# Every fourth K/V half transfer in two parts, of 120 and of 8 partitions

## The chip, the core and the metric

The kernel runs on one core of a Trainium2 chip: TensorE (PE) for matrix products, VectorE (DVE), ScalarE (ACT), GpSimd (POOL), and SyncE (SP), which here issues every DMA. 16 DMA engines carry the transfers between HBM and the core's SBUF, a memory of 128 partitions. The metric is the device time of one execution in microseconds (us), lower is better.

## What is computed

Two layers of decoding attention, each followed by a dense block, for 8 sequences with one new token each (model width 448). The attention has 16 query heads over 8 K/V heads of width 256, and sees the last 1024 of 4096 cached positions:

```python
k = jnp.repeat(k_cache[:, :, Sk - W:, :], rep, axis=1)
v = jnp.repeat(v_cache[:, :, Sk - W:, :], rep, axis=1)
scores = jnp.einsum("bhqd,bhkd->bhqk", q, k) * (Dh ** -0.5)
p = _softmax(scores, axis=-1)
o = jnp.einsum("bhqk,bhkd->bhqd", p, v)
...
x = x + _A_ref(_layernorm(x, axis=-1), A_k_cache, A_v_cache, A_wq, A_wo)
x = x + _B_ref(_layernorm(x, axis=-1), B_w1, B_w2)
x = x + _A_ref(_layernorm(x, axis=-1), A_k_cache, A_v_cache, A_wq, A_wo)
x = x + _B_ref(_layernorm(x, axis=-1), B_w1, B_w2)
```

`_B_ref` is a product with `w1`, a SiLU and a product with `w2`. Both layers use the same caches and weights, so the data of one sequence can be read once and used by both.

## The kernel before

The kernel is a plan: helpers record tasks (a few instructions of one engine, with an estimated duration and the names of what they read and write), `Plan.schedule` puts the tasks of PE, DVE, ACT and POOL in an order by these estimates, and `Plan.emit` writes the orders out with semaphore waits. SP's tasks keep the order in which they were recorded. Each DMA task names a semaphore of its own kind (for K and V one per slot and half). `emit` counts 16 for each DMA on it (L215), the DMA adds 16 when it has landed (L266), and whoever needs the data waits for the count (L261).

For each of the 8 sequences (`b`), the K data of 8 heads and then the V data of 8 heads come in. One head's K or V for 1024 positions is 512 KB and fills one of `R = 29` slots in SBUF, of 128 partitions by 2048 bf16. `load_k` (L522) and `load_v` (L528) fetch it as two halves of 128 partitions by 1024 elements, one row of 2 KB for each partition; for K a half is half of every row, for V it is half of the positions. That makes 8 x 16 x 2 = 256 halves of 256 KB. The weights (wq, wo, w1, w2) are loaded once, wq first and the others after the first sequence's K and V.

Two things hold a transfer of the stream back. `dma` (L476) makes it wait for the landing of the transfer recorded `AHEAD = 7` before it (L478), so that about seven are in flight. And `pump` (L981) records a load into a slot only behind the compute that used the slot before: both layers' scores for K, both layers' PV products for V.

Compute for one sequence: `layer1` transposes the K halves in place on DVE (L998), then come scores (L672), softmax, PV (L731) and the output projection (L774, L780); `layer2` runs the dense block of the first layer, the query projection (L877) and the second attention over the same slots. The dense block behind the second layer is done for seven sequences together near the end, and for the last sequence at the very end.

Of the kernel before, what the change touches and what calls it, by code (L numbers as in the profile page):

```python
# [32 lines left out]
class Plan:  # L33
# [10 lines left out]
    def add(self, eng, fns, reads=(), writes=(), dur=0.1, prio=0.0, name="", n_bytes=0, dma_key=None):  # L44
        if not isinstance(fns, (list, tuple)):
            fns = [fns]
        if eng == "pool":
            writes = list(writes) + ["pool_serial"]
        t = Task(eng, list(fns), dur, prio, name, n_bytes)
        t.idx = len(self.tasks)  # L50
        t.sem = dma_key
        deps = {}

        def dep(o, raw):
            if o is not t:
                deps[o.idx] = (o, raw or (deps[o.idx][1] if o.idx in deps else False))

        for k in reads:
            if k in self.last_w:
                dep(self.last_w[k], True)  # L60
            if k[0] == "bank":
                for r in self.readers.get(k, ()):
                    if r.eng != eng:
                        dep(r, False)
        for k in writes:
            if k in self.last_w:
                dep(self.last_w[k], True)
            for r in self.readers.get(k, ()):
                dep(r, False)
        for k in reads:  # L70
            if k not in writes:
                self.readers.setdefault(k, []).append(t)
        for k in writes:
            self.last_w[k] = t
            self.readers[k] = []
        t.deps = deps
        self.tasks.append(t)
        return t
# [116 lines left out]
    def emit(self):  # L195
        nc = self.nc
        order = self.order
        mk = nc.alloc_semaphore
        eng_sem = {e: mk("s_" + e) for e in ("pe", "dve", "act", "pool")}
        dsem, dcount = {}, {}  # L200
        for t in self.tasks:
            for o, raw in t.deps.values():
                if o.eng != t.eng or o.eng == "sp" or (raw and t.eng in ("dve", "act", "pool")):
                    o.users += 1
        cnt = {e: 0 for e in eng_sem}
        for e in eng_sem:
            for t in order[e]:
                if t.users:
                    cnt[e] += 1
                t.sem, t.val = e, cnt[e]  # L210
        for t in order["sp"]:
            if t.sem not in dsem:
                dsem[t.sem] = mk("s_d_" + t.sem)
                dcount[t.sem] = 0
            dcount[t.sem] += 16  # L215
            t.val = dcount[t.sem]
        handles = dict(eng_sem)
        handles.update(dsem)
        known = {e: {} for e in order}
        waits_of = {}  # L220
        pos = {e: 0 for e in order}
        n_done = 0
        total = len(self.tasks)
        emitted = set()
        while n_done < total:
            moved = False
            for e in order:
                while pos[e] < len(order[e]):
                    t = order[e][pos[e]]
                    if any(o.idx not in emitted for o, _ in t.deps.values()):  # L230
                        break
                    kn = known[e]
                    need = {}
                    for o, raw in t.deps.values():
                        if o.eng == e and e != "sp" and not (raw and e in ("dve", "act", "pool")):
                            continue
                        if need.get(o.sem, (0, None))[0] < o.val:
                            need[o.sem] = (o.val, o)
                    waits = []
                    for s, (v, o) in sorted(need.items(), key=lambda kv: -len(kv[1][1].vc)):  # L240
                        if kn.get(s, 0) >= v:
                            continue
                        waits.append((s, v))
                        kn[s] = v
                        for s2, v2 in o.vc.items():
                            if kn.get(s2, 0) < v2:
                                kn[s2] = v2
                    waits_of[t.idx] = waits
                    t.vc = dict(kn)
                    t.vc[t.sem] = max(t.vc.get(t.sem, 0), t.val)  # L250
                    emitted.add(t.idx)
                    pos[e] += 1
                    n_done += 1
                    moved = True
            assert moved, "the order of the engines is circular"

        def run_all(e):
            def f(eng):
                for t in order[e]:
                    for s, v in waits_of[t.idx]:  # L260
                        eng.wait_ge(handles[s], v)  # L261
                    ins = None
                    for fn in t.fns:
                        ins = fn(eng)
                    if e == "sp":
                        ins.then_inc(handles[t.sem], 16)  # L266
                    elif t.users:
                        ins.then_inc(handles[e], 1)
                if e == "sp":
                    eng.wait_ge(handles[order["sp"][-1].sem], order["sp"][-1].val)  # L270
            return f

        with nc.Block(no_gpsimd_drain=True) as block:
            block.sync(run_all("sp"))
            block.tensor(run_all("pe"))
            block.vector(run_all("dve"))
            block.scalar(run_all("act"))
            block.gpsimd(run_all("pool"))


def bass_interleave_layers__sliding_block_cached__dense_activation_silu__decode_kernel(
# [3 lines left out]
    _, HKV, SK, DH = A_k_cache.shape  # L285
# [3 lines left out]
    W = min(4096, max(256, SK // 4))  # L289
    S0 = SK - W  # L290
    P = 128
# [12 lines left out]
    HQ = 4.0 / D  # L304
    R = 29
    AHEAD = 7
    NJ = 3

    x2 = A_x.rearrange("b s d -> (b s) d")
# [7 lines left out]
    slots = [sb(f"slot{i}", [P, 2048], BF16) for i in range(R)]  # L317
# [158 lines left out]
    def dma(fn, writes, n_bytes, key, reads=(), rate=395e3, ahead=None):  # L476
        t = add("sp", fn, reads=reads, writes=writes, n_bytes=n_bytes, dma_key=key, dur=n_bytes / rate, name=key)
        if ahead and len(started) >= ahead:  # L478
            t.deps[started[-ahead].idx] = (started[-ahead], True)
        started.append(t)  # L480
# [37 lines left out]
    W1_R = [("w1", c) for c in range(5)] + ["w1_pad"]  # L518

    slot_of = {}  # L520

    def load_k(s, b, kvh):  # L522
        src = A_k_cache[b, kvh, S0:SK, :].rearrange("(p u) d -> p (u d)", p=P)
        for h in range(2):
            dma(lambda e, h=h: e.dma_start(slots[s][:, 1024 * h:1024 * h + 1024], src[:, 1024 * h:1024 * h + 1024]),
                [("slot", s, h)], W * DH, "slot%d_%d" % (s, h), ahead=AHEAD)

    def load_v(s, b, kvh):  # L528
        src = A_v_cache[b, kvh, S0:SK, :].rearrange("(h p u) d -> h p (u d)", h=2, p=P)
        for h in range(2):  # L530
            dma(lambda e, h=h: e.dma_start(slots[s][:, 1024 * h:1024 * h + 1024], src[h]),  # L531
                [("slot", s, h)], W * DH, "slot%d_%d" % (s, h), rate=378e3, ahead=AHEAD)

    def wq_l(o, i):
        if i < 3:
# [237 lines left out]
    def rows_part(i0, n, first, last, w_sb, rhs, reads, name):  # L773
        pe([lambda e, i=i, c=c: e.matmul(  # L774
            bank[XB][32 * c:32 * c + 1, 0:D], rhs(i), w_sb[:, i * D:(i + 1) * D],
            start=(first and i - i0 < 4), stop=(last and i - i0 >= n - 4), tile_position=(0, 32 * c),
            skip_group_check=True) for i in range(i0, i0 + n) for c in [i % 4]], reads, bk(XB), (D, 4), name)
# [203 lines left out]
    def pump():  # L981
        while n_load[0] < len(seq) and (n_load[0] < R or seq[n_load[0] - R] in freed):
            x = seq[n_load[0]]
            slot_of[x] = n_load[0] % R
            n_load[0] += 1
            (load_k if x[1] == "k" else load_v)(slot_of[x], x[0], x[2])
            if x == (0, "v", 7):
                load_wo()
                load_w1()
                load_w2()  # L990

    def layer1(b):
# [11 lines left out]
        for h in range(2):  # L1004
            rows_part(8 * h, 8, h == 0, False, wo_sb, lambda i: oT1[:, i % 2, i // 2:i // 2 + 1],
                      [("oT1", k) for k in (2 * h, 2 * h + 1)] + WO_R, "wor")
        pv_rows(b, 0, 1, oT1, "oT1", SC[0], 0, 0, NJ)
        if NJ:
            rows_part(16, 4*NJ, False, NJ == 3, wo_sb, lambda i: oT1[:, i % 2, i // 2:i // 2 + 1],
                  [("oT1", k) for k in range(4,4+NJ)] + WO_R, "wor")  # L1010
        for kvh in range(4+NJ, 8):
            pv_cols(b, 0, kvh, oT1, "oT1")
# [69 lines left out]
```

## Time and profile before

| | us |
|---|---|
| time, median of 3 runs | 270.83 (269.54 to 271.26) |
| the profiled execution | 269.46 |
| span of its trace, first to last instruction | 267.7 |
| PE busy | 210.4 (79%) |
| DVE busy | 153.8 (57%) |
| ACT busy | 75.0 (28%) |
| POOL busy | 21.0 (8%) |

The profile is of one execution. Its page gives busy times by engine, a picture of the span in 40 equal slices of 6.7 us (each digit the busy share in tenths), the DMA queues, and the chain of work that ended last, followed back from the last instruction. Busy digits of the DMA row are the mean over the 16 DMA engines; it can read a little over 1. "SPq" is the time SP spends on issuing. "x256" behind a group is a count. A wait is written as who waited, then an arrow to who released it, then the total, the number of times and the longest.

### The profile page before, as it was taken

To read this page: it belongs to the slowest core of one execution; us is meant where nothing else is said; L and a number is where in the kernel's file an instruction comes from. 1 tells how busy PE (TensorE), PEld (TensorE's weight loads), DVE (VectorE), ACT (ScalarE), POOL (GpSimd) and SP (SyncE) were. 2 spreads that over 40 slices of the span, in tenths; PEclk is the share of its full clock that TensorE was granted. 3 is DMA by queue.
4 is the path that set the end of the run, shared out by engine and by line. 5 is a ranking of instruction groups with operands and counts; after the bars stand their busy time and mean duration, and the time that the engine had idled before them with its cause. 6 is when DMAs were issued, how large, how long until landed. Compare 5 with 4: busy or idle time off the path is not lost.

```text
span 267.7 us, 11667 instructions
## 1 busy us (share of the span) xinstructions
PE 210.4 (79%) x5178; PEld 135.7 (51%) x5178; DVE 153.8 (57%) x453; ACT 75.0 (28%) x259; POOL 21.0 (8%) x115
## 2 busy tenths in 40 slices
PE   0054684778789878987899889769889985999996
PEld 0052341354457545654566556446555752667763
DVE  7289110156927880986498479818773891334233
ACT  2004310211053314332432533143343312430322
POOL 6100000002000200020002001000200020003000
PEclk9999999689999997999999999999999999999689
DMA  6999999999999999997999998999999998100000
GB/s 248 343 403 392 385 333 401 319 334 354 351 351 298 373 349 348 376 366 249 353 382 348 315 369 296 375 303 354 383 311 337 343 351 272 39 6 2 5 2 4
DMA packets 41123, 78.44 MB, mean 293 GB/s; under 512 B 4321, under 2 KB 7345, under 8 KB 40689
## 3 DMA queue, kind: packets, MB, share of 16 engines
q1 hardware_dynamic: 41072, 77.69, 82.3%
q8 instruction: 41, 0.67, 1.0%
q14 instruction: 10, 0.07, 0.1%
HBM read 77.67 MB, written 0.01 MB: 290 GB/s over the span
## 4 chain that ended last, share of the span: by engine, by line
PE 41%; DMA 35%; DVE 9%; SPq 6%; ACT 5%; issue 3%; ACTq 0%
DMA slot<-in_A_k_cache_dram 24%; PE bank L731 7%; PE bank L672 7%; DMA slot<-in_A_v_cache_dram 6%; DMA w2o<-in_A_wo_dram 6%; PE bank L774 5%; PE bank L877 5%; DVE slot L998 5%; SPq L531 4%; PE bank L833 3%; PE bank L780 3%; PE bank L1045 2%; DVE qT L882 2%; PE bank L558 2%; PE bank L888 2%
## 5 line engine op out<-in xcount | busy, mean ns | idle before, releaser
L998 DVE STREAM_TRANSPOSE slot<-slot 128x512 uint32<-128x512 uint32 x128 | 81.7, 684 | 11.4 <-DMA slot<-in_A_k_cache_dram 11.4
L672 PE MATMUL bank<-slot,qbd 128*8 128x256 bf16 x1024 | 38.2, 283 | 9.1 <-DVE mseg L678 4.5
L731 PE MATMUL bank<-slot,pT_sb 128*2 128x256 bf16 x960 | 41.7, 297 | 3.8 <-DMA slot<-in_A_v_cache_dram 2.7
L672 PEld LDWEIGHTS bank<-slot,qbd 128*8 128x8 bf16 x1024 | 23.4, 86 | 19.9 <-DVE mseg L678 6.4
L1045 PE MATMUL bank<-wq_sb,cols_b 128*32 128x512 bf16 (+2 forms) x269 | 29.7, 422 | 0.0
L731 PEld LDWEIGHTS bank<-slot,pT_sb 128*2 128x2 bf16 x960 | 22.4, 88 | 12.3 <-issue 5.2
L656 ACT ACTIVATE qbd<-q1s 32x128 bf16<-32x128 bf16 x32 | 10.1, 314 | 51.6 <-PE bank L672 51.0
L717 DVE RECIPROCAL rl_sb<-bank 128x16 f32<-128x16 f32 x16 | 4.1, 256 | 33.1 <-PE bank L712 33.0
L736 ACT ACTIVATE o_sb<-bank 128x256 bf16<-128x256 f32 x32 | 12.3, 383 | 35.9 <-PE bank L731 20.1
L774 PE MATMUL bank<-w2o,oT 128*1 128x448 bf16 x256 | 15.6, 359 | 6.9 <-issue 4.3
L877 PE MATMUL bank<-wq_sb,xn 128*4 128x256 bf16 (+1 forms) x384 | 18.7, 307 | 1.4 <-issue 0.9
L790 ACT ACTIVATE qT<-bank 128x448 bf16<-128x448 f32 x17 | 9.3, 544 | 28.0 <-PE bank L774 28.0
L566 POOL TENSOR_SCALAR rstd<-va 128x1 int32<-128x1 int32 x8 | 1.5, 192 | 195.3 <-ACT va L823 195.3
L678 DVE TENSOR_REDUCE mseg<-bank 128x1 f32<-128x256 f32 x32 | 12.8, 405 | 6.2 <-PE bank L672 6.0
L882 DVE STREAM_TRANSPOSE qT<-bank 128x256 f32<-128x256 f32 (+1 forms) x24 | 11.9, 521 | 7.7 <-PE bank L877 7.7
L833 PE MATMUL bank<-xbt,w_sb 128*128 128x32 bf16 x504 | 15.8, 177 | 0.1
L833 PEld LDWEIGHTS bank<-xbt,w_sb 128*128 128x128 bf16 x504 | 14.0, 97 | 2.0 <-ACT xbt L801 1.7
L742 DVE TENSOR_TENSOR oT<-bank,rl_sb 128x16 bf16<-128x16 f32 (+1 forms) x32 | 6.0, 186 | 15.0 <-PE bank L738 14.9
L1045 PEld LDWEIGHTS bank<-wq_sb,cols_b 128*32 128x32 bf16 (+2 forms) x269 | 9.1, 105 | 8.4 <-issue 5.6
L774 PEld LDWEIGHTS bank<-w2o,oT 128*1 128x1 bf16 x256 | 5.3, 82 | 12.3 <-DVE oT L742 4.8
L819 DVE SCALAR_TENSOR_TENSOR va<-bank,m 128x1 f32<-128x1 f32 x9 | 1.3, 149 | 17.0 <-ACT m L817 16.8
L695 ACT ACTIVATE qT<-bank,mb,rstd 128x256 bf16<-128x256 f32 x16 | 8.7, 565 | 7.0 <-DVE mb L691 6.8
(164 smaller groups left out, 267.6 us busy)
## 6 DMA issues: line engine op xcount, KB each, us to landing
slot<-in_A_k_cache_dram SPq DMA_DIRECT2D x128, 256.0 KB, 5.3
slot<-in_A_v_cache_dram SPq DMA_DIRECT2D x128, 256.0 KB, 5.2
w2o<-in_A_wo_dram SPq DMA_DIRECT2D x2, 1792.0 KB, 12.7
wq_sb<-in_A_wq_dram SPq DMA_DIRECT2D x3, 1024.0 KB, 7.0
w2o<-in_B_w_dram SPq DMA_DIRECT2D x1, 1568.0 KB, 15.5
w_sb<-in_B_w_dram SPq DMA_DIRECT2D x3, 448.0 KB, 13.9
wq_sb<-in_A_wq_dram SPq DMA_DIRECT2D x2, 256.0 KB, 10.3
w_sb<-in_B_w_dram SPq DMA_DIRECT2D x1, 128.0 KB, 12.7
```

Of the source, the lines that this page charges most:

```text
L531: dma(lambda e, h=h: e.dma_start(slots[s][:, 1024 * h:1024 * h + 1024], src[h]), [("slot", s, h)], W * DH, "slot%d_%d" % (s, h), rate=378e ...
L656: act(lambda e, q=q: e.activation(qbd[0][32 * q:32 * q + 32].rearrange("p k c (q r) -> p (k c) q r", r=2)[:, :, q, :], q1s[32 * t:32 * t + ...
L672: fns.append(lambda e, cb=cb, par=par, j=j, kvh=kvh, kv=kv: e.matmul(bank[sc][32 * j:32 * j + 8, k2 * 256:(k2 + 1) * 256], qbd[layer][:, k ...
L678: dve(lambda e: e.tensor_reduce(mseg[layer][:, k2:k2 + 1], bank[sc][:, k2 * 256:(k2 + 1) * 256], AX.X, ALU.max, negate=True), bk(sc), [("m ...
L731: fns.append(lambda e, qh=qh, uh=uh, j=j, vv=vv: e.matmul(bank[ob][32 * j:32 * j + 2, c0:c0 + DH], p_col(ei, k2, j, qh, uh), vv, start=(qh ...
L736: act(lambda e: e.activation(o_sb[oi][:], bank[ob][:, c0:c0 + DH], ACTF.Copy), bk(ob), [("o", oi)], 0.385, "oevh" if ob == OB[0] else "oev ...
L774: pe([lambda e, i=i, c=c: e.matmul(bank[XB][32 * c:32 * c + 1, 0:D], rhs(i), w_sb[:, i * D:(i + 1) * D], start=(first and i - i0 < 4), sto ...
L833: pe([lambda e, i=i, k=k, o=o: e.matmul(bank[XB][:, C_W1 + o * CW:C_W1 + o * CW + CW], w1_l(o, i), xbt[:, k:k + 1].broadcast_to([P, CW]), ...
L877: fns.append(lambda e, j=j, c=c, wb=wb, off=off, h0=h0, n=n, k2=k2: e.matmul(bank[wb][32 * j:32 * j + 4, h0:h0 + n], xn[:, part(c, k2), j, :],
L882: dve(lambda e, wb=wb, h0=h0, n=n: e.transpose(qT[:, h0:h0 + n].rearrange("p (c a i) -> p c a i", a=2, i=32), bank[wb][:, h0:h0 + n].rearr ...
L998: dve(lambda e, v=v: e.transpose(v, v), [("slot", s, h)], [("slot", s, h)], 0.67, "KT")
L1045: fills = {n: [lambda e, j=j, m=P // n: e.matmul(bank[OB[0]][m * j:m * j + m, 0:2 * DH], zero_b.broadcast_to([P, m]), wq_sb[:, 0:2 * DH], ...
```

## The change

A new helper `half` records the DMA task of a K or V half. It counts the halves, and every fourth of them (`SPARE = 4`) becomes a task of two DMAs, one for partitions 0 to 119 and one for partitions 120 to 127. Each head takes two halves, so the fourth is always the second half of every second head: 64 of the 256. Both DMAs of a task add 16 to the same semaphore, so `emit` now counts 16 for each DMA of a task, and a consumer waits for 32 more than before the task. The rates that the planner reckons with (395e3 for K, which was the default, and 378e3 for V) are as before, and a split half still counts as one task among the seven ahead.

```diff
-            dcount[t.sem] += 16
+            dcount[t.sem] += 16 * len(t.fns)
...
                     for fn in t.fns:
                         ins = fn(eng)
-                    if e == "sp":
-                        ins.then_inc(handles[t.sem], 16)
-                    elif t.users:
+                        if e == "sp":
+                            ins.then_inc(handles[t.sem], 16)
+                    if e != "sp" and t.users:
                         ins.then_inc(handles[e], 1)
...
+    SPARE = 4
...
+    n_half = [0]
+
+    def half(s, h, src, rate):
+        d = slots[s][:, 1024 * h:1024 * h + 1024]
+        n_half[0] += 1
+        cuts = [(0, 120), (120, P)] if n_half[0] % SPARE == 0 else [(0, P)]
+        dma([lambda e, a=a, z=z: e.dma_start(d[a:z], src[a:z]) for a, z in cuts],
+            [("slot", s, h)], W * DH, "slot%d_%d" % (s, h), rate=rate, ahead=AHEAD)
 
     def load_k(s, b, kvh):
         src = A_k_cache[b, kvh, S0:SK, :].rearrange("(p u) d -> p (u d)", p=P)
         for h in range(2):
-            dma(lambda e, h=h: e.dma_start(slots[s][:, 1024 * h:1024 * h + 1024], src[:, 1024 * h:1024 * h + 1024]),
-                [("slot", s, h)], W * DH, "slot%d_%d" % (s, h), ahead=AHEAD)
+            half(s, h, src[:, 1024 * h:1024 * h + 1024], 395e3)
```

`load_v` changes in the same way.

More of the change, by code (lines that the diff above doesn't have):

```diff
@@ L530, in load_v @@
         for h in range(2):
-            dma(lambda e, h=h: e.dma_start(slots[s][:, 1024 * h:1024 * h + 1024], src[h]),
-                [("slot", s, h)], W * DH, "slot%d_%d" % (s, h), rate=378e3, ahead=AHEAD)
+            half(s, h, src[h], 378e3)
     def wq_l(o, i):
```

## The prediction

> **What bounds the kernel now.** I read the page first (the slices, the queues, the chain by engine, the issues), then the stages, then what the DMA queue of SP waits for, then the chain in order of time.
>
> ```profile
> span 267.7 us, 11667 instructions
> ...
> DMA  6999999999999999997999998999999998100000
> GB/s 248 343 403 392 385 333 401 319 334 354 351 351 298 373 349 348 376 366 249 353 382 348 315 369 296 375 303 354 383 311 337 343 351 272 39 6 2 5 2 4
> ...
> q1 hardware_dynamic: 41072, 77.69, 82.3%
> q8 instruction: 41, 0.67, 1.0%
> ...
> PE 41%; DMA 35%; DVE 9%; SPq 6%; ACT 5%; issue 3%; ACTq 0%
> ...
> slot<-in_A_k_cache_dram SPq DMA_DIRECT2D x128, 256.0 KB, 5.3
> slot<-in_A_v_cache_dram SPq DMA_DIRECT2D x128, 256.0 KB, 5.2
> ```
>
> The DMA row stands at nine tenths or more in nearly every slice up to the 34th, about 227 us, and then falls to nothing; the rest is the last batch's compute. Of the 77.69 MB the 256 K/V halves of 256 KB are 67 MB. So the kernel is a stream of K/V halves with a tail of some 40 us. The chain gives PE more (41%) than DMA (35%), so I looked at whether the stream has slack:
>
> ```profile
> 6.00:10.00 4.00, 0.48 (x12) 0.40 (x12) 2.59 (x14) 0.05 (x1) 1.40 (x9) 1.00 1.02 426
> 10.50:12.30 1.80, 0.00 (x0) 0.00 (x0) 0.00 (x0) 0.00 (x0) 0.00 (x0) 1.00 1.00 236
> 14.00:20.00 6.00, 3.73 (x132) 3.52 (x130) 5.56 (x10) 0.00 (x0) 0.00 (x0) 1.00 1.06 405
> ...
> 60.00:200.00 140.00, 120.28 (x3054) 77.13 (x3050) 98.04 (x268) 46.62 (x166) 11.55 (x60) 0.99 0.98 343
> 200.00:225.00 25.00, 22.30 (x580) 14.50 (x572) 16.06 (x44) 7.75 (x28) 1.92 (x10) 1.00 0.95 328
> ```
>
> In each row the last two numbers are the mean busy share of the 16 DMA engines and the GB/s. Where K halves run with little else (14 to 20 us) the share is 1.06; in the long middle it is 0.98. At most (1.06 - 0.98) / 1.06 = 7.5% of the engines' time is idle there: all sixteen are near their limit, and PE (120 of 140 us) is close behind. What holds the queue back:
>
> ```profile
> SPq L525 <- DMA slot<-in_A_v_cache_dram: 11.2, 27, 1.8
> SPq L531 <- DMA slot<-in_A_v_cache_dram: 11.1, 27, 1.1
> SPq L525 <- DMA slot<-in_A_k_cache_dram: 9.9, 33, 0.7
> SPq L531 <- DMA slot<-in_A_k_cache_dram: 8.1, 23, 1.1
> SPq L531 <- PE bank L877: 5.8, 4, 2.1
> SPq L261 <- DMA slot<-in_A_k_cache_dram: 5.4, 15, 1.3
> SPq L261 <- DMA slot<-in_A_v_cache_dram: 2.8, 9, 0.5
> SPq L525 <- PE bank L731: 1.3, 4, 0.4
> ```
>
> These are SP's waits from 60 to 200 us. 48.5 us (the six DMA rows) go to the landing of the transfer seven earlier, 7.1 us (the two PE rows) to slots that the compute has not freed. So the landing of whole transfers paces the stream, and compute now and then.
>
> **The change, part by part.** Nothing moves on PE, VectorE, ScalarE or GpSimd: their orders are made by the planner from durations and dependencies that stay the same, and a consumer still waits for one semaphore, at a value 16 higher for each split before it. On SP every fourth half becomes two issues, 64 issues more in 320. A semaphore can't be passed early, because both parts of the last use must have added their 16.
>
> *SP's time.* The rows:
>
> ```profile
> L525 SPq DMA_DIRECT2D slot<-in_A_k_cache_dram x128: 327/328/1507, 3.9 to 211.3; - x128
> ...
> L482 SPq DMA_DIRECT2D slot<-in_A_x_dram x1: 385/385/385, 0.7 to 0.7; - x1
> ...
> 30.56 0.43 SPq L531
> ...
> 123.36 0.43 SPq L531
> ...
> 147.29 1.63 SPq L531
> ...
> 197.50 0.43 SPq L531
> 197.93 0.04 issue
> 197.97 0.43 SPq L531
> 198.40 0.04 issue
> 198.44 0.43 SPq L531
> 198.88 0.04 issue
> 198.92 6.22 DMA slot<-in_A_k_cache_dram
> 205.14 0.02 issue
> 205.16 5.50 DMA slot<-in_A_k_cache_dram
> ```
>
> An issue takes 0.33 us, also one of eight partitions (L482, 0.39), and in a burst one follows the other after 0.43 + 0.04 = 0.47 us. 64 more cost 64 x 0.47 = 30 us of SP; some three quarters of that, 22 us, fall in the 140 us in which SP waits 48.5 us for landings anyway, so on average they are hidden. Queued behind a small issue are the issues of the next halves, for which VectorE's transposes (K) and TensorE's PV (V) wait in the end. They show where SP sends a burst after slots came free: the chain has such bursts near 30, 122, 147 and 197 us (its SPq share is 6%, 16 us). Each has about six issues, so one more each: 4 x 0.47 = 1.9 us. The bounds are 0 (landings still order the burst) and a quarter of 16 us, 4 us.
>
> *The small part.* Eight rows of 2 KB. The page's q1 row gives what a row costs: 0.823 x 16 x 267.7 us / 41072 = 86 ns of one DMA engine. The lower bound is that each of the eight goes to an engine of its own beside the main part: the fullest engines get one row more per split, 64 x 86 ns = 5.5 us. The trace has nothing as narrow as eight partitions, but it has transfers of 64:
>
> ```profile
> 2.53 1.37 SPq L489 DMA_DIRECT2D wq_sb<-in_A_wq_dram  x2
> ...
> DMA to landing us min/median/max: 10.2/10.3/10.4
> ```
>
> These two are issued at 2.53 to 3.90 us and land 10.3 us later, around 13 us; the stage 10.50:12.30 is mostly theirs. The engines are as busy there (1.00) and move 236 GB/s, against 405 in 14:20 with 128 partitions. Engines held fully at 0.58 of the rate mean that a row takes 86 x 405 / 236 = 147 ns when it shares few partitions with others. By 147 ns, 64 small parts cost 64 x 0.147 = 9.4 us. The upper bound scales the rate on to eight partitions: 236 x 8 / 64 = 29.5 GB/s, 16.4 KB in 0.56 us, 64 x 0.56 = 35.5 us. I take 9.4 us, from the row as measured: it is the nearest transfer of the trace, and the further step to eight is tempered by there being only eight rows, one at a time among full-width traffic. A gain here is excluded: the same bytes move in more pieces.
>
> [...]
>
> *The main part.* 120 rows. If they load each engine as a full half does, or less, nothing is added: 0, at best 1/16 of 0.65 us (256 KB at 405 GB/s) back, 64 x 0.04 = 2.6 us. If its rows go at 147 ns instead of 86, eight rows in turn add 8 x 61 ns = 0.49 us, 64 times 31 us. I take 0, since 120 partitions are far nearer to 128 than to 64.
>
> *What the slack gives back.* A slower stream finds more slots free: of the 7.1 us that SP waits for PE I take half, 3.6 us, off the cost.
>
> *Sum.* 9.4 + 1.9 - 3.6 = +7.7 us. The profiled execution took 269.46 us, 267.7 of it the span, so it would come to 277.2. The three runs have a median of 270.83 (269.54 to 271.26), 1.4 above the profiled one, and the forecast stands on that median: 278.5 us.
>
> **The rivals.** *Faster: one engine is the straggler.* The cut at 120 looks like taking work from the engine that serves the last eight partitions. The q8 row gives a reason: 41 instruction fetches hold 1.0% of 16 engines' span, 43 us, or 1.04 us each, as long as twelve rows. Were they all on that one engine, 64 x 8 rows x 86 ns = 44 us taken off would balance it just so. Against it: an engine with 43 us more than the rest would leave the other fifteen idle for that time, some 20% of the 220 us, and the share would be near 0.85; it is 0.98. So at most the 7.5% of idleness can be won, 12 us of the 165 us from 60 to 225, less 5.5 us for the rows that others get: 6.5 us, 264.3. It decides if the idleness is nearly all a wait for one engine. [...] Chance 0.13.
>
> *Same: hidden.* The idle 2 to 11% of engine time takes up 5.5 us of rows, SP's slack takes the issues, and the waits for slots the rest: 0 to 2 us, about 271.5. For it speaks that much of the chain from 57 to 196 us is compute. Chance 0.22.
>
> *Much slower: the main part is narrow too.* It decides if its rows land in each other's way as those of the 64 do: up to 31 us more, 309.5; half of it gives 294. Chance 0.12.
>
> **How the numbers follow.** My own case, slower by 3 to 15 us (273.5 to 286), has 0.53; its point is 278.5. The range leaves out the faster rival and the worse half of the last one, and takes in the hidden case: 269 to 294. A change under 1%, 2.7 us, is what a measurement of this kernel can't tell from none. Faster by over 1%: 0.13. Within: 0.22. Slower: 0.53 + 0.12 = 0.65.
>
> **What would show it.** Right: the DMA share stays near 0.98 from 60 to 200 us at fewer GB/s than 343, K and V land later than 5.3 and 5.2 us after their issue, and the stream's end moves from 227 to about 235 us with the tail of 40 us unchanged. The small part's own landing beside the main part's tells its price, and SP's DMA waits should shrink by about 20 us. Wrong: GB/s over 343 at a share that rises to 1.06 means that one engine was the straggler. An unchanged end with longer SP issue bursts means that the slack hid it. A main part that lands far later than a whole half means the last rival.

## The result, and the profile after

| | before | with the change |
|---|---|---|
| time, median of 4 runs each | 270.19 us (267.34 to 271.26) | 306.0 us (304.72 to 308.83) |
| ratio | | 1.1359, 95% interval 1.1238 to 1.1479 |
| the profiled execution, and its span | 269.46, 267.7 | 308.83, 307.0 |

An execution can be some per cent slower than another one of the same kernel; a ratio with an interval compares the faster executions alone, so it need not be the quotient of the medians beside it.

The change makes the kernel 36 us slower, some 4.6 times the 7.7 us that the prediction summed to, and beyond its range of 269 to 294 us. The page of the changed kernel: the DMA share and what the engines moved in 40 slices (now 7.7 us each), the queues, the chain by engine, the issues.

```profile
span 307.0 us, 11720 instructions
...
DMA  7999999999999999999999999999999999300000
GB/s 266 344 331 320 290 338 378 343 289 286 282 291 293 288 284 280 275 290 289 280 284 276 275 291 292 301 282 284 287 306 279 310 298 295 104 5 2 4 2 1
DMA packets 41570, 78.43 MB, mean 255 GB/s; under 512 B 4768, under 2 KB 7792, under 8 KB 41136
...
q1 hardware_dynamic: 41520, 77.69, 86.1%
...
DMA 74%; PE 19%; issue 2%; SPq 2%; ACT 2%; DVE 1%; ACTq 0%
...
slot<-in_A_k_cache_dram SPq DMA_DIRECT2D x96, 256.0 KB, 6.2
slot<-in_A_v_cache_dram SPq DMA_DIRECT2D x96, 256.0 KB, 6.1
slot<-in_A_k_cache_dram SPq DMA_DIRECT2D x32, 240.0 KB
slot<-in_A_v_cache_dram SPq DMA_DIRECT2D x32, 240.0 KB
```

The bytes are the same (77.69 MB on q1) and the engines are as full, but from the ninth slice on they move 275 to 310 GB/s. Whole halves, which the change does not touch, land after 6.2 and 6.1 us instead of 5.3 and 5.2. The chain is DMA for 74%, where PE had the larger share. The stream ends in the 35th slice, near 264 us, and the tail behind it is some 40 us as before. The q1 row has 448 packets more, 7 for each of the 64 cuts.

In the traces these are packets of 4 bytes, 4320 before and 4768 with the change. A whole half has 16 of them (2901 beside 23210 rows of 2 KB from 60 to 200 us before, so 16 to 128 rows), a part of 8 rows has 8 (the small parts alone, below: 4832 packets under 512 B on the page, 4320 without those 64 parts), and so a part of 120 rows has 15: 15 + 8 - 16 = 7. How many engines a part uses no view tells.

The stages, with share and GB/s as the last two numbers:

```profile
14.00:20.00 6.00, 3.60 (x128) 3.38 (x124) 5.03 (x9) 0.00 (x0) 0.00 (x0) 1.00 1.06 344
...
60.00:200.00 140.00, 108.74 (x2531) 67.21 (x2534) 83.90 (x220) 36.37 (x130) 9.54 (x50) 0.89 1.02 287
```

In the middle the engines are fuller than before (1.02, was 0.98) and move less (287 GB/s, was 343): a byte takes (1.02 / 287) / (0.98 / 343) = 1.24 times as much engine time. The first stage, with nothing but K halves, has the same share of 1.06 and 344 in place of 405. So it is the transfers that became slower, not the work around them. SP's waits in the middle:

```profile
SPq L528 <- DMA slot<-in_A_v_cache_dram: 23.6, 54, 1.0
SPq L528 <- DMA slot<-in_A_k_cache_dram: 23.2, 52, 0.9
SPq L261 <- DMA slot<-in_A_k_cache_dram: 9.0, 15, 2.2
SPq L261 <- DMA slot<-in_A_v_cache_dram: 6.5, 8, 1.0
...
SPq L528 <- PE bank L884: 0.5, 2, 0.3
```

62.3 us of waits for landings of K and V halves (48.5 before), although SP issues more; the waits for slots have nearly gone. SP is not the bound.

### The profile page after: what moved, and what is told of

It reads as the page before. It is cut to its first block, busy times and chain, and to the rows that moved or that the text cites. A ratio compares the mean times of both kernels' runs of the same rounds, so it can differ in the third digit from the quotient of the medians.

```text
span 307.0 us, 11720 instructions
## 1 busy us (share of the span) xinstructions
PE 227.0 (74%) x5167; PEld 141.0 (46%) x5178; DVE 156.2 (51%) x453; ACT 75.0 (24%) x259; POOL 20.8 (7%) x115
## 2 busy tenths in 40 slices
DMA packets 41570, 78.43 MB, mean 255 GB/s; under 512 B 4768, under 2 KB 7792, under 8 KB 41136
## 3 DMA queue, kind: packets, MB, share of 16 engines
q1 hardware_dynamic: 41520, 77.69, 86.1%
## 4 chain that ended last, share of the span: by engine, by line
DMA 74%; PE 19%; issue 2%; SPq 2%; ACT 2%; DVE 1%; ACTq 0%
DMA slot<-in_A_k_cache_dram 34%; DMA slot<-in_A_v_cache_dram 33%; DMA w2o<-in_A_wo_dram 5%; PE bank L781 4%; PE bank L738 4%; DMA wq_sb<-in_A_wq_dram 2%; PE bank L840 2%; PE bank L565 1%; PE bank L1052 1%; SPq L528 1%; PE bank L884 1%; PE bank L787 1%; PE bank L679 1%; ACT qT L797 1%; PE bank L798 0%
## 5 line engine op out<-in xcount | busy, mean ns | idle before, releaser
L1005 DVE STREAM_TRANSPOSE slot<-slot 128x512 uint32<-128x512 uint32 x128 | 84.2, 690 | 20.7 <-DMA slot<-in_A_k_cache_dram 19.9
L738 PE MATMUL bank<-slot,pT_sb 128*2 128x256 bf16 x960 | 49.9, 330 | 16.9 <-DMA slot<-in_A_v_cache_dram 15.2
L679 PE MATMUL bank<-slot,qbd 128*8 128x256 bf16 x1024 | 39.8, 291 | 11.9 <-DVE mseg L685 5.9
L738 PEld LDWEIGHTS bank<-slot,pT_sb 128*2 128x2 bf16 x960 | 24.0, 93 | 30.9 <-issue 16.3
L781 PE MATMUL bank<-w2o,oT 128*1 128x448 bf16 x256 | 21.4, 457 | 10.9 <-DVE oT L749 6.3
L1052 PE MATMUL bank<-wq_sb,cols_b 128*32 128x512 bf16 (+2 forms) x258 | 27.8, 448 | 1.0 <-issue 1.0
L884 PE MATMUL bank<-wq_sb,xn 128*4 128x256 bf16 (+1 forms) x384 | 19.6, 325 | 0.5
L781 PEld LDWEIGHTS bank<-w2o,oT 128*1 128x1 bf16 x256 | 6.1, 96 | 19.6 <-issue 9.1
L895 PE MATMUL bank<-qT,irep 128*128 128x64 f32 x32 | 7.9, 336 | 3.0 <-DVE qT L889 2.5
```

What stands on the lines that cost most here:

```text
L679: fns.append(lambda e, cb=cb, par=par, j=j, kvh=kvh, kv=kv: e.matmul(bank[sc][32 * j:32 * j + 8, k2 * 256:(k2 + 1) * 256], qbd[layer][:, k ...
L738: fns.append(lambda e, qh=qh, uh=uh, j=j, vv=vv: e.matmul(bank[ob][32 * j:32 * j + 2, c0:c0 + DH], p_col(ei, k2, j, qh, uh), vv, start=(qh ...
L781: pe([lambda e, i=i, c=c: e.matmul(bank[XB][32 * c:32 * c + 1, 0:D], rhs(i), w_sb[:, i * D:(i + 1) * D], start=(first and i - i0 < 4), sto ...
L884: fns.append(lambda e, j=j, c=c, wb=wb, off=off, h0=h0, n=n, k2=k2: e.matmul(bank[wb][32 * j:32 * j + 4, h0:h0 + n], xn[:, part(c, k2), j, :],
L1005: dve(lambda e, v=v: e.transpose(v, v), [("slot", s, h)], [("slot", s, h)], 0.67, "KT")
L1052: fills = {n: [lambda e, j=j, m=P // n: e.matmul(bank[OB[0]][m * j:m * j + m, 0:2 * DH], zero_b.broadcast_to([P, m]), wq_sb[:, 0:2 * DH], ...
```

## The experiments

Times are medians; the kernel before ran on the same chip each time, and its median stands beside them. Where a ratio to it was taken, it follows with its interval. The kernel before spread by 6 to 11 us in each group of runs (263 to 274 us in one), so a few us between two medians are not settled.

**Without the small part.**

```diff
-        cuts = [(0, 120), (120, P)] if n_half[0] % SPARE == 0 else [(0, P)]
+        cuts = [(0, 120)] if n_half[0] % SPARE == 0 and n_load[0] > R else [(0, P)]
```

> Every fourth half is one transfer of partitions 0 to 119 and the part of 8 is left out, for the 50 of 64 that reuse a slot (the first 29 slots are filled whole; the last 8 rows then hold older data). [...] Theory S (the part of 8 does it, 16 KB in 0.56 us): back to 266 to 272 us. Theory L (two issues and a later second landing empty the window of seven): one issue again, 266 to 271 us.

Measured: 294.35 us beside 272.39. One issue for each half, no small part, and 22 us slower for 50 cuts, in proportion 28 us for 64, and rows took 110 ns in the mean (the table below, 92 before): the ranges of theories S and L are out. In later expectations theory N is that the main part carries the loss and that slow rows hold the engines, and this run is in accord with it. The page's rows of this kernel show it setting in:

```profile
GB/s 261 350 403 389 359 386 336 379 313 359 323 292 292 294 299 284 290 293 282 277 279 285 280 290 260 321 307 290 301 305 308 301 286 280 94 3 5 2 5 1
...
q1 hardware_dynamic: 40622, 76.87, 85.4%
...
slot<-in_A_k_cache_dram SPq DMA_DIRECT2D x104, 256.0 KB, 6.1
slot<-in_A_v_cache_dram SPq DMA_DIRECT2D x102, 256.0 KB, 5.8
slot<-in_A_v_cache_dram SPq DMA_DIRECT2D x26, 240.0 KB, 6.1
slot<-in_A_k_cache_dram SPq DMA_DIRECT2D x24, 240.0 KB, 6.3
```

A slice is 7.3 us. While slots are still filled whole the rates are those of before (403 in the third slice); from the twelfth slice on, about 80 us, when slots are loaded again and every fourth half has 120 rows, they stay around 290. A part of 120 rows lands hardly later than a whole half. The q1 row has 450 packets fewer than before, 9 for each cut: the 8 rows left out and one more, as a part of 120 rows has 15 small packets and not 16.

**Cut at 112.**

```diff
-        cuts = [(0, 120), (120, P)] if n_half[0] % SPARE == 0 else [(0, P)]
+        cuts = [(0, 112), (112, P)] if n_half[0] % SPARE == 0 else [(0, P)]
```

> [...] Theory L: two issues, 300 to 308 us.

Measured: 300.08 us beside 272.39. Its q1 row has 42096 packets, 16 more than before for each cut, so its two parts have 32 small packets between them where those of 120 and 8 rows have 23, and it is nearly as slow: the loss does not need the fewer small packets. Its middle stage:

```profile
60.00:200.00 140.00, 117.30 (x2691) 71.52 (x2688) 87.19 (x232) 40.85 (x143) 9.55 (x50) 0.88 1.03 306
```

**Cut by columns.**

```diff
-        cuts = [(0, 120), (120, P)] if n_half[0] % SPARE == 0 else [(0, P)]
-        dma([lambda e, a=a, z=z: e.dma_start(d[a:z], src[a:z]) for a, z in cuts],
+        cuts = [(0, 512), (512, 1024)] if n_half[0] % SPARE == 0 else [(0, 1024)]
+        dma([lambda e, a=a, z=z: e.dma_start(d[:, a:z], src[:, a:z]) for a, z in cuts],
```

> Every fourth half is cut by columns instead, into two transfers of 128 partitions by 512 elements (rows of 1 KB): as many issues, semaphore steps and landings as the change has, all of them 128 partitions wide. [...] Theory L: 300 to 308 us, as the change.

Measured: 273.94 us beside 272.39. As many issues and landings as the change, at 335 GB/s:

```profile
60.00:200.00 140.00, 121.95 (x2977) 77.27 (x2981) 96.05 (x258) 44.03 (x158) 11.30 (x59) 0.95 0.99 335
```

Theory L is out. By the medians 64 more issues cost about 1.5 us; beside the fastest run of the kernel before (265.39) it would be 8 to 9, so only the order of size is known.

**Cut at 64.** The same edit with 64 for 120.

> [...] Theory N by the stage of 64-partition transfers (236 GB/s against 405): 256 KB take 1.1 us instead of 0.65, 64 x 0.46 = 29 us, 290 to 305 us. [...] Theory L: 300 to 308 us.

Measured: 306.03 us beside 272.39, with 289 GB/s in the middle:

```profile
60.00:200.00 140.00, 110.36 (x2554) 66.59 (x2551) 85.33 (x227) 38.84 (x138) 9.54 (x50) 0.90 1.02 289
```

That is a little over theory N's 290 to 305; the price that the 64-partition stage gave, 29 us for 64 cuts, was near the 33.6 measured.

**The small part alone.** It needs room, so both kernels have 28 slots.

```diff
-    R = 29
+    R = 28
...
+        fns = [lambda e: e.dma_start(d, src)]
+        keys = [("slot", s, h)]
+        if n_half[0] % SPARE == 0:
+            i = n_half[0] // SPARE % 2
+            fns.append(lambda e: e.dma_start(scr[120:P, 1024 * i:1024 * i + 1024], src[120:P]))
...
```

> The kernel before with 28 slots instead of 29, the control for the next run, which needs the room of a slot. All theories: 270 to 276 us, since the landings pace the stream more than the slots.

> 28 slots, every half whole, and with every fourth a second transfer of its last 8 rows to a spare area of the same partitions: the small part alone, as 1 MB more. Theory S as the prediction took it (147 ns for a row): 9 us over the run with 28 slots; by its upper bound 36 us over it. Theory N (the main part carries the cost): 4 to 10 us over it.

Measured: 273.01 us with 28 slots, 274.22 with the small parts, ratios to the kernel before of 1.0125 (1.0058 to 1.0192) and 1.011 (1.0061 to 1.0158). The intervals lie over each other: by whole transfers the small part costs nothing that can be measured, less than either theory gave it. With 28 slots the engines have a little more idle time, though, in which it can hide (a share of 0.95 in the middle, 0.98 with 29):

```profile
60.00:200.00 140.00, 118.72 (x2955) 76.62 (x2961) 93.84 (x255) 43.78 (x158) 11.30 (x59) 0.95 0.95 327
60.00:200.00 140.00, 117.69 (x2974) 76.81 (x2978) 95.46 (x259) 44.01 (x159) 11.46 (x60) 0.98 0.97 339
```

The first row is that of 28 slots alone, the second that with the small parts.

**Both parts again, in the same 50 halves as the run without the small part.**

```diff
-        cuts = [(0, 120), (120, P)] if n_half[0] % SPARE == 0 else [(0, P)]
+        cuts = [(0, 120), (120, P)] if n_half[0] % SPARE == 0 and n_load[0] > R else [(0, P)]
```

> The change with its cuts (120 and 8, both loaded) in the same 50 halves as the run that left the small part out. Theory M (the main part carries nearly all): 295 to 300 us, within 4 us of the run without the small part on the same chip. Theory C (the small part costs little by whole transfers but more in the company of the main part): 300 to 306 us, 6 to 10 us over it.

> The run without the small part once more, on the chip of the run beside it: 292 to 297 us in both theories.

Measured: 299.01 us with both, 1.1287 (1.1107 to 1.1467), and 295.17 without the small part, 1.1001 (1.0704 to 1.1297), beside 270.84. Between the two lie 3.8 us by the medians, as theory M has it, and by the ratios 0.0286 of some 265 us, 7.6 us, as theory C has it. The intervals overlap, so which of the two holds stays open. The kernel without the small part also loads 0.8 MB less, an estimated 2.8 us at the 290 GB/s of this stretch. Either way the main part carries most of the loss: 24.3 of 28.2 us by the medians, 0.1001 of 0.1287 by the ratios.

**Even and odd partitions.** Two parts of 64 rows, one with partitions 0, 2, 4 and so on, one with the others.

```diff
-        cuts = [(0, 120), (120, P)] if n_half[0] % SPARE == 0 else [(0, P)]
-        dma([lambda e, a=a, z=z: e.dma_start(d[a:z], src[a:z]) for a, z in cuts],
+        cuts = [(0, 2), (1, 2)] if n_half[0] % SPARE == 0 else [(0, 1)]
+        dma([lambda e, a=a, z=z: e.dma_start(d[a::z], src[a::z]) for a, z in cuts],
```

> Every fourth half is cut into the even and the odd partitions, two transfers of 64 rows that both span all 128 partitions. Theory W (what counts is how much of the partition range a part spans, half of it for the parts cut at 64): 272 to 280 us. Theory A (what counts is which rows each engine gets, so that rows of two engines meet): 290 to 306 us, as the cut at 64.

> The cut into even and odd partitions once more, beside the runs above and timed in three rounds. Theory A: rows at their old speed and only the issues to pay, 271 to 277 us. Theory W2 (half the rows in a transfer always cost): 278 to 286 us.

Measured: 281.66 us beside 269.69, and in three rounds 280.96 us, 1.0486 (1.0378 to 1.0594). Theory A's 290 to 306 us are out. The time is a little over what theory W allowed, and in the second run it is that of W2. The trace of the second run does not bear W2 out. First its stages, then its chain and the issues of whole halves, then SP's waits from 60 to 200 us:

```profile
14.00:20.00 6.00, 3.73 (x132) 3.51 (x130) 5.77 (x10) 0.00 (x0) 0.00 (x0) 1.00 1.06 402
60.00:200.00 140.00, 117.66 (x2896) 74.97 (x2888) 91.84 (x251) 43.85 (x155) 9.63 (x50) 0.94 0.95 325
```

```profile
DMA 33%; PE 33%; SPq 16%; DVE 11%; issue 4%; ACT 3%; ACTq 0%
...
slot<-in_A_k_cache_dram SPq DMA_DIRECT2D x96, 256.0 KB, 4.8
slot<-in_A_v_cache_dram SPq DMA_DIRECT2D x96, 256.0 KB, 4.7
```

```profile
SPq L528 <- DMA slot<-in_A_v_cache_dram: 2.3, 6, 0.7
...
SPq L261 <- DMA slot<-in_A_k_cache_dram: 1.8, 5, 0.7
...
SPq L528 <- DMA slot<-in_A_k_cache_dram: 1.3, 2, 0.8
```

The engines keep their pace: 402 GB/s where K halves run alone (344 with the change), idle time left (0.95), whole halves that land sooner than before (4.8 us). SP waits for landings only 5.4 us (and 0.3 in a row not shown) instead of 48.5, and its issues are 16% of the chain. So here the issuing is late, not the transfers. The issues of K, in ns (least, median, most), for the even and odd cut, the columns and the cut at 64:

```profile
L528 SPq DMA_DIRECT2D slot<-in_A_k_cache_dram x160: 327/477/1362, 4.0 to 220.5; - x160
L528 SPq DMA_DIRECT2D slot<-in_A_k_cache_dram x160: 327/430/1511, 3.8 to 216.5; - x160
L528 SPq DMA_DIRECT2D slot<-in_A_k_cache_dram x160: 327/472/1422, 4.0 to 244.0; - x160
```

The median was 328 ns before. The cut at 64 has issues as long as this one, so it is not the step between partitions that makes them long. Whether these longer issues make up all of the 12 to 13 us was not tried.

**All halves cut at 120.**

```diff
-    SPARE = 4
+    SPARE = 1
```

> All 256 halves are cut at 120. Theory own (each cut transfer costs its time by itself, about 0.5 us): 270 + 256 x 0.55 = 410 us. Theory mix (the cost is where rows of cut transfers meet rows of whole ones, and is less where all are cut alike): 280 to 340 us.

Measured: 317.27 us beside 269.69. Theory own is out by far. The time lies in the range of theory mix, but the engines are less full in the middle, at 282 GB/s, so part of the loss is not slow rows:

```profile
60.00:200.00 140.00, 105.12 (x2500) 65.36 (x2508) 79.04 (x214) 36.67 (x133) 8.09 (x42) 0.89 0.94 282
```

For theory mix speaks that a byte takes (0.94 / 282) / (0.98 / 343) = 1.17 times the engine time of before, less than the 1.24 with a quarter of the halves cut.

**Every eighth half.** `SPARE = 8`.

> Every eighth half is cut, 32 in place of 64. Theory own (each cut transfer costs its time by itself): half of 36 us, 286 to 290 us. Theory mix (rows of cut transfers put those of the whole ones out of step, which lasts beyond the cut one): more than half, 292 to 300 us.

Measured: 277.75 us beside 270.84, 7 us for 32 cuts. In time that is less than theory own, and the opposite of theory mix.

```profile
60.00:200.00 140.00, 121.10 (x2953) 77.60 (x2965) 95.49 (x258) 44.68 (x159) 11.39 (x59) 0.94 1.00 336
```

The share is 1.00 instead of 0.98 and the rate 336 instead of 343: part of what 32 cuts cost went into idle engine time.

**Ten in flight.** `AHEAD = 10`.

> The change with ten transfers in flight instead of seven. Theory N (the DMA engines are held by slow rows): no gain, 303 to 310 us, and a landing that takes longer by the three more in front. Theory L (the window of seven empties behind a late second part): back to 275 to 285 us.

Measured: 310.52 us beside 270.84, 1.1736 (1.1391 to 1.2081). That is no gain; whole halves land later, and no more:

```profile
slot<-in_A_k_cache_dram SPq DMA_DIRECT2D x96, 256.0 KB, 9.1
slot<-in_A_v_cache_dram SPq DMA_DIRECT2D x96, 256.0 KB, 8.5
```

**Neighbours, and every sixth half.**

```diff
-    SPARE = 4
+    SPARE = 8
...
-        cuts = [(0, 120), (120, P)] if n_half[0] % SPARE == 0 else [(0, P)]
+        cuts = [(0, 120), (120, P)] if n_half[0] % SPARE < 2 else [(0, P)]
```

For every sixth half it is `SPARE = 6` alone.

> 64 halves are cut at 120 as in the change, but as neighbours, two in every eight, so that six whole transfers lie between the pairs where the change has three. Theory number (each cut transfer takes its share of the engines, and 32 were hidden by the idle time that the engines had left): as the change, 300 to 308 us. Theory spacing (rows go on colliding for several transfers after a cut one, and come to rest only if enough whole ones follow): 280 to 292 us.

> Every sixth half is cut, 42. Theory number: 10 more than the 32 that cost 7 us, at the (36 - 7) / 32 = 0.9 us of the next 32, 284 to 289 us. Theory spacing: five whole transfers between two, fewer than the seven in flight, so nearer to the change than by number, 290 to 302 us.

Measured: the pairs 294.44 us, 1.0974 (1.0838 to 1.111); every sixth 288.34 us, 1.0747 (1.058 to 1.0914); both beside 267.91. So 32, 42 and 64 cuts cost 7, 20 and 36 us, and 64 in pairs 26.5. Every sixth lies where theory number had it in time, but its 20 us over the kernel before are more than the 16 that it gave; the pairs lie between the theories. Both the number and the spacing have a part, and how they share it in time stays open; the rows below show more of it.

**Cut at 96.** The same edit with 96 for 120.

> [...] Theory A (which rows each engine gets, when they are not spread over the 128 partitions as those of a whole half): 295 to 308 us. Theory D (the numbers 120, 112 and 8 don't divide well): 270 to 276 us.

Measured: 302.78 us beside 267.91, 1.1285 (1.1139 to 1.1431): theory A's range. 96 and 32 divide by 16 and 32, and it is as slow:

```profile
60.00:200.00 140.00, 110.49 (x2581) 66.72 (x2573) 84.44 (x225) 39.78 (x140) 9.62 (x50) 0.91 1.03 293
```

## Why the prediction was wrong

**What bounds the kernel** was right: the stream paces it, the engines had at most 7.5% idle, and the time grew by about as much as the end of the stream moved (from some 229 to 264 us).

**The main part** is the step that failed. The prediction put it at 0, "since 120 partitions are far nearer to 128 than to 64". The runs show no such scale: cuts at 120, 112, 96 and 64 cost 36, 28, 35 and 34 us. Without its small part the main part costs 22 to 24 us for 50 cuts by the medians, in proportion 28 to 31 for 64. The upper bound that stood in the same paragraph, 31 us, was near this size, and the rival built on it, "the main part is narrow too" (309.5 us, chance 0.12), came nearest with its time. In part that is luck: the 31 us were the price of the cut rows alone, and the traces show that rows of whole halves paid too (below). The sign set for that rival, a main part that lands far later than a whole half, did not show either (6.1 and 6.3 us against 5.8 and 6.1): all transfers landed later.

**The small part** was put at 9.4 us. Alone it costs about 1 us, which is not clear of the noise. In the company of the main part it costs 4 to 8 us for 50 cuts (5 to 10 for 64), its bytes included, so there the 9.4 are not refuted. The rate of the narrow stage was used on the small part, while most of the loss lay in the main one. The rows of that stage were misread besides: 256 KB over 64 partitions are rows of 4 KB, which took 274 ns each in the trace, so 137 ns for 2 KB and not 147.

**SP's issues**, 1.9 us: about 1.5 by the medians of the cut into columns, which has as many. **The slack**, 3.6 us given back: the waits for slots did go, but so did all the idle engine time, and it could not show against 36 us.

**The signs.** Landings came later, at fewer GB/s, and the tail stayed 40 us, as said. The share rose from 0.98 to 1.02 instead of staying, since rows hold their engines longer (115 ns instead of 92, below). SP's waits for landings grew by 14 us instead of shrinking by 20, because the landings fell behind by more than the issues took.

**The rivals.** The faster one took the last eight partitions to be the work of one engine. No view names the engine of a row, so that was not shown. Nothing was won by taking their rows off: with them left out of 50 halves the kernel took 294.35 us beside 272.39.

**What makes it slow** is shown up to a point. It isn't the issues (columns), the number of small packets (41072 + 64 x 16 = 42096 packets on q1 at 112, 96 and 64, and as many with even and odd partitions), the window of seven (ten in flight), nor that a part has few rows (even and odd). The trace of each run keeps the time of every packet, which no view prints one by one, and a row of 2 KB is one packet. Of those that started from 60 to 200 us:

| kernel | rows under 90 ns | mean of a row, ns |
|---|---|---|
| before | 96% | 92 |
| columns (rows of whole halves) | 95% | 94 |
| small parts alone, 28 slots | 95% | 92 |
| even and odd partitions (second run) | 94% | 95 |
| every eighth half cut at 120 | 76% | 96 |
| every sixth at 120 | 56% | 104 |
| 64 halves at 120, in pairs | 57% | 105 |
| every fourth at 120 (the change) | 19% | 115 |
| all halves at 120 | 33% | 107 |
| every fourth, cut at 112 | 36% | 108 |
| every fourth, cut at 96 | 21% | 114 |
| every fourth, cut at 64 | 25% | 114 |
| 120 rows alone, 50 halves (first run) | 34% | 110 |

With the change only a quarter of the rows belongs to cut halves, but four fifths are slow, so most rows of whole halves are slow too. And the slow rows do not follow the number of cuts: 24% of all with every eighth half cut and 81% with every fourth, but 43% when the same 64 cuts stand in pairs. The time follows the rows: 4, 12, 13 and 23 ns more for the mean row go with 7, 20, 26.5 and 36 us (every eighth, every sixth, pairs, every fourth). Nor are whole halves needed for it: with all halves cut, two thirds of the rows are slow.

Slow were the kernels with parts of 64 to 120 neighbouring partitions (96 to 115 ns for the mean row); parts spread over all 128 were not (95), and neither were eight neighbouring rows alone beside whole halves (92). Neither a view nor the trace names the engine of a row or the place it goes to. So neither which rows each engine gets (theory A) nor that rows land in each other's way (the last rival) is shown, and no run separates the writing into SBUF from the reading of HBM, which a cut can change as well. What holds the rows up stays open.

## What to carry to other kernels

Beside a stream of full 128-partition transfers, a transfer over 64 to 120 neighbouring partitions was not just a smaller transfer here: with every fourth half cut, 64% to 81% of all rows took 90 ns or more (4% before), so those of the whole halves in flight with it were slow too. If a transfer must be cut, cut it by columns: that took 273.94 us beside 272.39. When a profile shows a narrow transfer at a lower rate with engines as full as ever (236 GB/s here, 405 at full width), don't scale that by the number of partitions: reckon with it for every large part that is not whole, and measure. And before work is taken off one engine, the mean share bounds what a straggler can be worth: with 0.98 here, and 1.06 in a full stage, at most 7.5%.

## What the runs showed of the hardware

Three things were not expected. The cost by number is far from a line: by the medians 32 cut transfers of 256 cost 7 us and 64 cost 36, and 24% and 81% of all rows are slow. Parts of 64 rows at every second partition left the engines their rate (402 GB/s in the K stage), while 64 neighbouring rows took it to 289 GB/s over the middle. And transfers of 8 rows, 64 of them with 1 MB in all, cost 1.2 us by the medians beside whole transfers, within the noise.
